# Two token blocks through w_in by Strassen's scheme, seven products instead of eight, with twelve weight slots

## The chip, the cores and the metric

One core of a Trainium2 chip runs the kernel. The metric is the device time of one execution in microseconds (us); the median of several runs is given. TensorE (PE in the rows) multiplies matrices into PSUM, which has eight banks of 128 x 512 fp32 values; VectorE (DVE), ScalarE (ACT) and GpSimd (POOL) do the rest, and SyncE (SP) issues the DMAs.

## The reference

Attention over four batches of eight heads, with 32 global tokens that see everything and 512 local ones that see a window of 32 and the global ones, gives 2176 tokens of 512 features. These go through two layers of the same form, in fp32:

```python
x = np.ascontiguousarray(attn_out.transpose(0, 2, 1, 3)).reshape(B * S, H * D)   # 2176 x 512
...
h = x @ w_in                 # 512 x 2048
r = np.maximum(h, 0.0)
g = r * r
return (g @ w_out).astype(np.float32)    # 2048 x 512
```

## The kernel before

Every operation is first entered in a plan (`add`: engine, estimated cost, priority, what it reads and writes). `order` then plays the plan through with its estimates, each engine taking the ready operation of the lowest priority number, and the operations are issued in the order that comes out. So each engine has one fixed order. Dependences follow the order in which operations were added: who writes a buffer waits for all who read it before.

Products are made precise by splitting: a value is stored as a high part (`xh`, `gh`, `whi`) in a rounded fp32 type (F32R) and the rest (`xl`, `gl`, `wlo`), and each product takes three matmuls: high by high, high weight by low value, low weight by high value (lines 509 to 511 and 534 to 536).

The tokens stand in five blocks of 256, 512, 512, 512 and 384 columns, numbered 0 to 4. A layer is cut into four waves of 512 hidden features; there are eight waves in all (`lw`), numbered 0 to 7, and a wave takes every block through `moe`. For each of four groups f of 128 hidden features, four groups k of 128 input features are accumulated in a bank (h or S, four of these); then `r` = relu on ScalarE, its square to `gh` on ScalarE, the same to `gf` on VectorE (line 523) and `gl` = `gf` - `gh` on VectorE (`minus`, line 218). Then w_out: four groups d of output features by four f, accumulated in four banks (Y, PT, PT, O), and added to `y` by VectorE (line 547; in a layer's first wave ScalarE copies instead). The last wave of the first layer splits y into the next layer's `xh` and `xl`, the last wave of the second stores y.

Weights come as 64-bit patterns in chunks of 512 KB, eight in a wave (four of w_in, four of w_out). `weight` loads one into `wraw` (there is one such buffer) and turns it into fp32 in `wt` by four VectorE operations and an absolute value that VectorE or ScalarE makes (lines 466 to 478); ScalarE writes the high part into a slot (line 484), and VectorE or GpSimd the low part (`minus`, 'wl'). There are 16 slots, two waves' worth; eight of them take the room of attention's buffers once attention is done (`arena`).

Attention (`pair`, 32 of them, and `glob`, 8) fills x block by block, and wave 0 of the first layer runs in between. From wave 1 on, banks and slots of attention are free for the rest. In the waves 1 to 6 the blocks run in the order 1, 2, 4, 0, 3, in the last in the order 1, 2, 3, 4, 0. Two activations can be under way (`r`, `gf`: two buffers each). The settings are in `CFG`: letters say which engine takes an operation (A ScalarE, D VectorE, P GpSimd), in turn.

Of the kernel before, what the change touches and what calls it, by code (L numbers as in the profile page):

```python
# [10 lines left out]
F32 = mybir.dt.float32  # L11
# [20 lines left out]
NSLOT = 16  # L32
CFG = {'EARLY': 8,
 'ck': 'PPP',
 'cq': 'P',
 'lo': 'D',
 'nm': 'AD',
 'ev': 'A',
 'yc': 'AA',
 'wl': 'DDPP',  # L40
 'gl': 'D',
 'xh': 'AADA',
 'glob': [5, 5, 13, 17, 19, 27, 31, 37],
 'w0': -1.361,
 'w1': 684422.049,
 'moe': [341.089, 23.225, 54.691, -112.195, -211.616],
 'step': [0.2638, 0.5671, 0.1425, 0.013, 0.2305],
 'NK': 3,
 'NQ': 3,
 'wa': 'DAA',  # L50
 'lid': -317.614,
 'lmk': -11.49,
 'gbuf': '01',
 'lead': 14.017,
 'NM': 2,
 'NS': 3,
 'NPT': 5,
 'NV': 2,
 'NR': 2,
 'NG': 2,  # L60
 'NWR': 1,
 'NWT': 2,
# [17 lines left out]
class Op:  # L80
    __slots__ = ("eng", "cost", "fn", "prio", "seq", "deps", "users", "left", "ready", "start", "end", "tail", "lock")


class Plan:
# [8 lines left out]
    def add(self, eng, cost, prio, fn, reads=(), writes=(), tail=0.0, lock=False):  # L93
        op = Op()
        op.eng, op.cost, op.prio, op.fn, op.tail, op.lock = eng, cost, prio, fn, tail, lock
        op.seq = len(self.ops)
# [23 lines left out]
    def order(self):  # L120
# [7 lines left out]
        done, dma, dmas, cols, port = [], 0.55, [], {}, {}  # L128
        while len(done) < len(self.ops):
# [14 lines left out]
            if e == "PE":  # L144
                n = int(t / TICK)
                if cols.get(n - 1, 0.0) < 3060:
                    op.end += op.cost * 0.95
# [23 lines left out]
        return done  # L171

# [14 lines left out]
def kernel(ctx: ExitStack, tc: tile.TileContext, kl, ql, vl, gk, gv, win, wout, msk, idn, out):  # L187
# [27 lines left out]
    def minus(key, prio, out_, a, b, n, reads, writes):  # L215
        get = lambda v: v() if callable(v) else v
        if pick(key) == "D":
            add("DVE", dve(n), prio, lambda: nc.vector.tensor_tensor(  # L218
                out=get(out_), in0=a, in1=get(b), op=ALU.subtract), reads, writes, lock=True)
        else:  # L220
            add("Pool", 0.25 + 0.0021 * n, prio, lambda: nc.gpsimd.tensor_tensor(  # L221
                out=get(out_), in0=a, in1=get(b), op=ALU.subtract), reads, writes)
# [14 lines left out]
    NR, NG, NWR, NWT = (CFG[k] for k in ("NR", "NG", "NWR", "NWT"))  # L237
    rt = tiles(big, "r", NR, [128, 512])
    gft = tiles(big, "gf", NG, [128, 512])
# [22 lines left out]
    late_opened = []  # L262

    def open_late():
        if not late_opened:
# [3 lines left out]
            for j in range(NSLOT - EARLY):  # L269
                whi.append(lp.tile([128, 512], F32R, name=f"whi{EARLY + j}"))  # L270
                wlo.append(lp.tile([128, 512], F32R, name=f"wlo{EARLY + j}"))

    bank = {k: ps.tile([128, 512], F32, name=k) for x in ("h", "Y", "S", "PT", "O") for k in CFG[x]}
    cnt = {"S": 0, "PT": 0, "g": 0, "h": 0, "Y": 0, "r": 0, "gf": 0}
# [10 lines left out]
    def pair(j, prio):  # L285
# [31 lines left out]
        add("PE", 0.86, P(), scores, A + (M, ML, HQ, LQ), tuple(sk))  # L317
        pbs = []
        ok = CFG["O"][j % len(CFG["O"])]
        for e in range(2):  # L320
# [31 lines left out]
            add("PE", 0.468, P(), trans, A + (("s", sb, 0), ("s", sb, 1), "ident"), (tk,))  # L352
# [13 lines left out]
        add("PE", 1.03, P(), pv, A + (("pt", pbs[0]), ("pt", pbs[1]), ("v", vb)), (ok,))  # L366
        b, c0 = UNIT_POS[u]
        split_out(b, [h2], xh[b][:, h2, c0:c0 + 256], xl[b][:, h2, c0:c0 + 256], ok, bank[ok][:, 0:256], 256, P)
# [8 lines left out]
    def glob(n, prio):  # L377
# [16 lines left out]
        for e in range(2):  # L394
# [7 lines left out]
            add("PE", 0.96, P(), scores, A + (GK,), (sk,))  # L402
# [20 lines left out]
        def trans():  # L423
# [3 lines left out]
        add("PE", 0.49, P(), trans, A + (GP, "ident"), (t1,))  # L427
        copy("ev", P(), kt[:, 0:512], bank[t1], 512, A + (t1,), (GK,), psum=True)
        add("PE", 0.15, P(), lambda: nc.tensor.transpose(bank[t2][0:32, 0:128], p[:, 512:544], ident),
            A + (GP, "ident"), (t2,))  # L430
# [12 lines left out]
        add("PE", 1.645, P(), pv, A + (GK, GV), (ok,))  # L443
# [7 lines left out]
    def weight(c, prio):  # L451
        w, r = divmod(c, 8)
        src = (win if r < 4 else wout)[4 * w + r % 4]
        slot, rb, tb = c % (NSLOT), c % NWR, c % NWT
        late = slot >= EARLY
        R, T = ("wraw", rb), ("wt", tb)
        q = [prio]

        def P():
            q[0] += 1e-3  # L460
            return q[0]

        low, high, t = wraw[rb][:, :, 0], wraw[rb][:, :, 1], wtmp[tb]
        tf = t.bitcast(F32)
        load(prio, wraw[rb].rearrange("p c t -> p (c t)"), src.bitcast(U32), 524288, (), (R,))
# [14 lines left out]

        def hi():
            if late:
                open_late()
            nc.scalar.activation(out=whi[slot], in_=tf, func=AF.Copy)  # L484

        W = (("w", slot),) + ((("arena",) if c < NSLOT else ()) if late else ())
# [198 lines left out]
```

## Time and profile before

| | |
|---|---|
| median of 3 runs | 904.36 us (904.07 to 904.84) |
| the profiled execution | 904.31 us, its span 902.5 us |
| TensorE busy | 888.0 us (98%) |
| VectorE, ScalarE, GpSimd busy | 577.3, 405.2, 80.7 us |
| read from HBM, written | 62.54 MB, 4.46 MB |

The span goes from the first instruction to the last; the 1.81 us between it and the execution's time lie around it. Busy times count how long an engine had an instruction under way. Matmuls overlap, so their lengths are longer than the distance from one to the next, and the distance is what counts. The same holds for VectorE's operations.

### The profile page before, as it was taken

The page shows a single profiled execution, that of the slowest core. Times are in us where ns is not written, and L with a number is a line of the kernel's source. Part 1 is how long each engine was busy: PE and PEld are TensorE (multiplying, and loading weights), DVE is VectorE, ACT ScalarE, POOL GpSimd, SP SyncE. Part 2 cuts the span into 40 slices and gives each one's busy share as a digit, 9 for nine tenths or more (in the row PEclk, how much of TensorE's full clock was granted, in tenths as well). Part 3 has the DMA queues.
Part 4 walks back from the last instruction along what each step waited for, and adds up shares of the span by engine and source line. Part 5 has one row for each costly group of instructions (what it writes and reads, how often), then busy time and mean ns, then how long its engine had stood idle before and what let it go on. Part 6 is the DMA issues. An engine that isn't in the chain of part 4 may idle for free.

```text
span 902.5 us, 14362 instructions
## 1 busy us (share of the span) xinstructions
PE 888.0 (98%) x5416; PEld 765.8 (85%) x5416; DVE 577.3 (64%) x1396; ACT 405.2 (45%) x933; POOL 80.7 (9%) x108
## 2 busy tenths in 40 slices
PE   6999999999999999999999999999999999999998
PEld 4878777778888988898889888998899889988888
DVE  6999989655567777765776675356645763333343
ACT  5989788755433333333344444454313332222221
POOL 2322221100110011001000001000100110000000
PEclk9999999999999999999999999999999999999999
DMA  9768634210222222221110012002200210001111
GB/s 313 249 196 251 193 106 134 81 32 1 70 71 64 59 89 71 70 70 47 52 66 24 24 60 80 25 24 71 69 25 2 70 47 1 1 1 48 47 47 59
DMA packets 28069, 67.92 MB, mean 75 GB/s; under 512 B 3168, under 2 KB 12512, under 8 KB 28000
## 3 DMA queue, kind: packets, MB, share of 16 engines
q1 hardware_dynamic: 28000, 67.01, 23.6%
q8 instruction: 42, 0.69, 0.3%
q14 instruction: 27, 0.22, 0.1%
HBM read 62.54 MB, written 4.46 MB: 74 GB/s over the span
## 4 chain that ended last, share of the span: by engine, by line
PE 92%; DVE 4%; ACT 2%; DMA 2%; issue 0%; SPq 0%; ACTq 0%
PE h L509 8%; PE h L510 7%; PE h L511 7%; PE S L510 6%; PE S L509 6%; PE S L511 6%; PE PT L534 6%; PE PT L536 6%; PE PT L535 6%; PE Y L534 5%; PE Y L536 4%; PE Y L535 4%; PE O L534 3%; PE O L535 3%; PE O L536 3%; PE O L362 3%
## 5 line engine op out<-in xcount | busy, mean ns | idle before, releaser
L519 ACT ACTIVATE r<-h 128x512 f32<-128x512 f32 (+2 forms) x88 | 46.8, 533 | 220.1 <-PE h L511 219.9
L509 PE MATMUL h<-xh,whi 128*128 128x512 f32 (+2 forms) x352 | 130.2, 370 | 0.7 <-DVE gf L523 0.7
L510 PE MATMUL h<-xl,whi 128*128 128x512 f32 (+2 forms) x352 | 126.4, 359 | 0.0
L511 PE MATMUL h<-xh,wlo 128*128 128x512 f32 (+2 forms) x352 | 126.1, 358 | 0.0
L218 DVE TENSOR_TENSOR gl<-gf,gh 128x512 fp32r<-128x512 f32 (+2 forms) x160 | 99.5, 623 | 21.5 <-ACT gh L521 10.4
L534 PE MATMUL PT<-gh,whi 128*128 128x512 f32 (+2 forms) x288 | 102.6, 356 | 0.0
L511 PE MATMUL S<-xh,wlo 128*128 128x512 f32 (+2 forms) x288 | 102.6, 356 | 0.0
L536 PE MATMUL PT<-gh,wlo 128*128 128x512 f32 (+2 forms) x288 | 102.6, 356 | 0.0
L510 PE MATMUL S<-xl,whi 128*128 128x512 f32 (+2 forms) x288 | 102.6, 356 | 0.0
L509 PE MATMUL S<-xh,whi 128*128 128x512 f32 (+2 forms) x288 | 102.6, 356 | 0.0
L535 PE MATMUL PT<-gl,whi 128*128 128x512 f32 (+2 forms) x288 | 102.6, 356 | 0.0
L523 DVE SCALAR_TENSOR_TENSOR gf<-h,r 128x512 f32<-128x512 f32 (+2 forms) x88 | 53.5, 609 | 73.5 <-ACT r L519 73.2
L521 ACT ACTIVATE gh<-r 128x512 fp32r<-128x512 f32 (+2 forms) x160 | 90.4, 567 | 6.4 <-PE Y L536 2.4
L221 POOL TENSOR_TENSOR wlo<-wt,whi 128x512 fp32r<-128x512 f32 x32 | 43.6, 1364 | 521.5 <-ACT whi L484 521.5
L534 PE MATMUL Y<-gh,whi 128*128 128x512 f32 (+2 forms) x208 | 76.6, 368 | 0.0
L509 PEld LDWEIGHTS h<-xh,whi 128*128 128x128 f32 x352 | 66.4, 189 | 11.1 <-DVE gf L523 0.9
L536 PE MATMUL Y<-gh,wlo 128*128 128x512 f32 (+2 forms) x208 | 74.6, 359 | 0.0
L535 PE MATMUL Y<-gl,whi 128*128 128x512 f32 (+2 forms) x208 | 74.6, 359 | 0.0
L511 PEld LDWEIGHTS h<-xh,wlo 128*128 128x128 f32 x352 | 66.5, 189 | 8.6
L510 PEld LDWEIGHTS h<-xl,whi 128*128 128x128 f32 x352 | 66.5, 189 | 7.8 <-DVE xl L373 0.2
L547 DVE TENSOR_TENSOR y<-y,Y 128x512 f32<-128x512 f32 (+2 forms) x30 | 18.2, 606 | 84.3 <-PE Y L536 84.2
L519 ACT ACTIVATE r<-S 128x512 f32<-128x512 f32 (+2 forms) x72 | 38.4, 533 | 67.8 <-PE S L511 65.2
(79 smaller groups left out, 1758.9 us busy)
## 6 DMA issues: line engine op xcount, KB each, us to landing
wraw<-win SPq DMA_DIRECT2D x32, 512.0 KB, 3.5
wraw<-wout SPq DMA_DIRECT2D x32, 512.0 KB, 3.5
v<-vl SPq DMA_DIRECT2D x32, 224.0 KB, 2.9
rk<-kl SPq DMA_DIRECT2D x32, 192.0 KB, 3.8
y<-gk SPq DMA_DIRECT2D x8, 672.0 KB, 6.1
y<-gv SPq DMA_DIRECT2D x8, 640.0 KB, 8.2
rq<-ql SPq DMA_DIRECT2D x32, 128.0 KB, 3.1
out<-y SPq DMA_DIRECT2D x12, 256.0 KB, 2.1
```

Source lines behind the costliest of these rows:

```text
L218: add("DVE", dve(n), prio, lambda: nc.vector.tensor_tensor(out=get(out_), in0=a, in1=get(b), op=ALU.subtract), reads, writes, lock=True)
L221: add("Pool", 0.25 + 0.0021 * n, prio, lambda: nc.gpsimd.tensor_tensor(out=get(out_), in0=a, in1=get(b), op=ALU.subtract), reads, writes)
L362: nc.tensor.matmul(out=bank[ok][64 * e:64 * e + 64, 128 * t:128 * t + 128], lhsT=vt[vb][:, 128 * k + 64 * e:128 * k + 64 * e + 64], rhs=pt ...
L509: nc.tensor.matmul(out=hp, lhsT=hi, rhs=xh[b][:, k, :], start=k == 0, stop=False)
L510: nc.tensor.matmul(out=hp, lhsT=hi, rhs=xl[b][:, k, :], start=False, stop=False)
L511: nc.tensor.matmul(out=hp, lhsT=lo, rhs=xh[b][:, k, :], start=False, stop=k == KD - 1)
L519: add("Activation", act(nb), P(), lambda r=r, hp=hp: nc.scalar.activation(out=r, in_=hp, func=AF.Relu), (hk,), (("r", ri),))
L521: add("Activation", act(nb) + 0.04, P(), lambda r=r, a=a: nc.scalar.activation(out=a, in_=r, func=AF.Square), (("r", ri),), (("gh", f),))
L523: add("DVE", dve(nb), P(), lambda r=r, hp=hp, gf=gf: nc.vector.scalar_tensor_tensor(out=gf, in0=hp, scalar=0.0, in1=r, op0=ALU.max, op1=AL ...
L534: nc.tensor.matmul(out=o, lhsT=hi, rhs=gh[f][:, 0:nb], start=f == 0, stop=False)
L535: nc.tensor.matmul(out=o, lhsT=hi, rhs=gl[f][:, 0:nb], start=False, stop=False)
L536: nc.tensor.matmul(out=o, lhsT=lo, rhs=gh[f][:, 0:nb], start=False, stop=f == 3)
```

## The change

In waves 1 to 7 blocks 1 and 2 no longer go through `moe` each for itself but together through `wino`, W in the orders. The two blocks, two halves of the input features (k 0, 1 and k 2, 3) and a pair of f make a 2 x 2 by 2 x 2 product of blocks; `products` computes it by seven products of six matmuls each, in Winograd's form of Strassen's scheme. For that

- four sums of the two blocks' x are made (`tsums`): T1 takes the place of block 2's first half, T2 to T4 have tiles of their own. It runs once before wave 1, from `xh` + `xl`, and once before the second layer, from y;
- each pair of w_in chunks gets four half sums (`sums`), which fill two more slots, split as the chunks are. A wave holds 4 + 4 + 4 = 12 slots, and there are 12;
- a bank B accumulates product after product, and is copied out in between (`keep`, ScalarE); two other banks take the products that are added to those copies (`plus`, VectorE). Three of the four results of a pair are thus in `r` buffers, of which there are now three, and go through `activate` with `staged` (VectorE squares in place, ScalarE copies to `gh`); `gf` is gone;
- w_out of blocks 1 and 2 is accumulated for two f at a time (`second`) and added to y twice in a wave.

The slots are given out from a list of free ones, in the order in which they are released. The orders of blocks are 340W, 3W04, W403, 4W30, W043, 0W43 and 3W40 for the waves 1 to 7. The planner now counts a cost for a change between kinds of matmul (`switch`), and many settings of attention are others: which engine casts, normalises and converts, how many buffers there are, and in which order wave 0, the loads and the `glob`s come. `visit` and `after` only rearrange code. Unchanged lines and most of the first part are left out:

```diff
-NSLOT = 16
+NSLOT = 12
+PB = (1, 2)
...
+ 'tl': 'D',
+ 'tp': [495.69, 306.05],
+ 'order': ['340W', '3W04', 'W403', '4W30', 'W043', '0W43', '3W40'],
...
- 'nm': 'AD',
+ 'nm': 'APA',
...
- 'wl': 'DDPP',
+ 'wl': 'DDDD',
...
- 'xh': 'AADA',
- 'glob': [5, 5, 13, 17, 19, 27, 31, 37],
...
+ 'xh': 'AAA',
+ 'glob': [6, 7, 13, 15, 19, 26, 27, 29],
...
- 'NQ': 3,
- 'wa': 'DAA',
...
+ 'NQ': 2,
+ 'wa': 'ADDA',
...
- 'NPT': 5,
+ 'NPT': 2,
...
- 'NR': 2,
- 'NG': 2,
+ 'lag': 6,
+ 'NR': 3,
...
- 'NWT': 2,
+ 'NWT': 3,
...
+    def sums(f0, f1, slots, P, arenas):
+
+        (t0, T0), (t1, T1) = f0, f1
+        half = lambda t, i: t[:, 256 * i:256 * i + 256]
+        for out_, a, b, op, rd, wr in (
+                (half(t0, 0), half(t0, 0), half(t1, 0), ALU.subtract, (T1,), T0),
+                (half(t1, 0), half(t1, 0), half(t1, 1), ALU.add, (), T1),
+                (half(t1, 1), half(t1, 1), half(t0, 0), ALU.subtract, (T0,), T1),
+                (half(t0, 1), half(t0, 1), half(t1, 1), ALU.subtract, (T1,), T0)):
+            add("DVE", dve(256), P(), lambda out_=out_, a=a, b=b, op=op: nc.vector.tensor_tensor(
+                out=out_, in0=a, in1=b, op=op), rd, (wr,), lock=True)
+        for s, (t, T) in zip(slots, ((t1, T1), (t0, T0))):
+            split(s, t, T, P, arenas[s])
...
+        for p in range(2):
+            t = [chunk("in", 2 * p + i) for i in range(2)]
+            ss = [slot() for _ in range(2)]
+            sums(t[0], t[1], [s for s, _ in ss], P, dict(ss))
+            res["sum"].append([s for s, _ in ss])
+            for i in range(2):
+                chunk("out", 2 * p + i)
...
+        if staged:
+            r, R = src, S
+            add("DVE", dve(nb), P(), lambda: nc.vector.scalar_tensor_tensor(
+                out=r, in0=r, scalar=0.0, in1=r, op0=ALU.max, op1=ALU.mult), (), (R,), lock=True)
+            add("Activation", act(nb) + 0.04, P(), lambda: nc.scalar.activation(out=a, in_=r, func=AF.Copy),
+                (R,), (("gh", f),))
...
+        def keep(i):
+            copy("sg", P(), s[i], B, nb, (kb,), (G[i],), psum=True)
+
+        def plus(i, hk, hp):
+            add("DVE", dve(nb), P(), lambda: nc.vector.tensor_tensor(out=s[i], in0=s[i], in1=hp, op=ALU.add), (hk,), (G[i],))
+
+        product(kb, B, f0, 0, x(b0, 0), True)
+        keep(0)
+        product(ka, A, f0, 2, x(b0, 2), True)
+        plus(0, ka, A)
+        activate(P, 0, nb, s[0], G[0], True)
+        product(kb, B, sa, 2 - 2, t(2), False, False) if False else product(kb, B, sa, 2, t(2), False)
+        keep(1)
+        product(kc, C, sa, 0, t(1), True)
+        product(kb, B, sb, 0, t(3), False)
+        keep(2)
+        plus(2, kc, C)
+        product(kb, B, f1, 2, t(4), False)
+        activate(P, 1, nb, B, kb, False)
+        product(kc, C, sb, 2, x(b1, 2), False)
+        plus(1, kc, C)
+        rest = lambda: (activate(P, 3, nb, s[2], G[2], True), activate(P, 2, nb, s[1], G[1], True))
...
+        r0 = products(W, 0, P)
+        r0()
+        release(*W["sum"][0])
+        st_ = lambda p: (layer, wave == 0 and p == 0, wave == WAVES - 1 and p == 1)
+        second(P, PB[0], (0, 1), o[0:2], True, True, st_(0))
+        r1 = products(W, 1, P)
+        release(*W["sum"][1])
+        second(P, PB[1], (2, 3), o[0:2], True, True, st_(0))
+        r1()
+        second(P, PB[0], (0, 1), o[2:4], True, True, st_(1))
+        second(P, PB[1], (2, 3), o[2:4], True, True, st_(1))
+        if free:
+            release(*W["in"], *W["out"])
...
+                whole(s0, S0, b1, 2 + i)
+                whole(s1, S1, b1, i)
+                tt(s0, s0, s1, ALU.subtract, (S1,), S0)
+                split_t(3, i, s0, S0)
+                whole(s2, S2, b0, i)
+                tt(s1, s1, s2, ALU.subtract, (S2,), S1)
+                split_t(1, i, s1, S1)
+                tt(s0, s0, s2, ALU.add, (S2,), S0)
+                split_t(2, i, s0, S0)
+                whole(s1, S1, b0, 2 + i)
+                tt(s1, s1, s0, ALU.subtract, (S0,), S1)
+                split_t(4, i, s1, S1)
```

## Rows read from the trace of the kernel before

**Rows 1.** The page: busy time of each engine; engines of the last chain
```profile
PE 888.0 (98%) x5416; PEld 765.8 (85%) x5416; DVE 577.3 (64%) x1396; ACT 405.2 (45%) x933; POOL 80.7 (9%) x108
...
PE 92%; DVE 4%; ACT 2%; DMA 2%; issue 0%; SPq 0%; ACTq 0%
```

**Rows 2.** Windows of stage one: stretch, length, then busy us of each engine
```profile
0.00:27.50 27.50, 18.85 (x127) 14.94 (x127) 19.70 (x78) 15.43 (x43) 6.22 (x15) 1.00 0.83 280
27.50:100.00 72.50, 71.69 (x821) 58.06 (x819) 69.14 (x295) 65.10 (x206) 18.68 (x33) 1.00 0.73 225
100.00:220.00 120.00, 118.43 (x988) 94.89 (x987) 85.73 (x333) 88.37 (x257) 17.82 (x32) 1.00 0.31 92
220.00:244.50 24.50, 24.50 (x121) 21.70 (x120) 15.87 (x30) 11.99 (x23) 2.58 (x2) 1.00 0.16 45
```

**Rows 3.** Windows, columns as in the group before: waves 1, 4 and 7
```profile
244.50:338.00 93.50, 93.50 (x488) 82.91 (x487) 66.68 (x116) 34.27 (x62) 8.03 (x6) 1.00 0.24 73
...
525.00:618.00 93.00, 93.00 (x480) 81.83 (x479) 50.38 (x87) 40.08 (x75) 5.76 (x4) 1.00 0.15 46
...
805.00:898.70 93.70, 93.70 (x482) 82.40 (x481) 36.79 (x61) 22.05 (x40) 0.00 (x0) 1.00 0.12 43
```

**Rows 4.** Timeline of TensorE, wave 1: start us, length us, line, output<-inputs
```profile
253.34 0.39 PE L509 MATMUL S<-xh,whi 128*128 128x512 f32 x1
...
254.70 0.39 PE L509 MATMUL S<-xh,whi 128*128 128x512 f32 x1
```

**Rows 5.** Waits of TensorE, line <- releaser: us in total, times, longest us
```profile
PE S L314 <- POOL hq L211: 4.8, 1, 4.8
PE S L314 <- DVE mn L326: 3.0, 1, 3.0
PE h L509 <- DVE gf L523: 0.7, 1, 0.7
```

**Rows 6.** Timeline, the end: the last matmul
```profile
898.71 0.28 PE L536 MATMUL O<-gh,wlo 128*128 128x256 f32 x1
```

**Rows 7.** Timeline of VectorE: operations of 512 columns, and one of 256
```profile
473.36 0.68 DVE L547 TENSOR_TENSOR y<-y,Y 128x512 f32<-128x512 f32 x1
...
476.96 0.68 DVE L547 TENSOR_TENSOR y<-y,O 128x512 f32<-128x512 f32 x1
...
494.22 0.43 DVE L218 TENSOR_TENSOR gl<-gf,gh 128x256 fp32r<-128x256 f32 x1
```

**Rows 8.** Timeline of VectorE, weight conversions in wave 1: L466 begins, L478 ends
```profile
247.13 0.43 DVE L466 TENSOR_SCALAR wt<-wraw 128x512 uint32<-128x512 uint32 x1 [2.12 <-DMA wraw<-wout]
...
319.81 0.69 DVE L478 SCALAR_TENSOR_TENSOR wt<-wraw,wt 128x512 f32<-128x512 f32 x1
324.13 0.43 DVE L466 TENSOR_SCALAR wt<-wraw 128x512 uint32<-128x512 uint32 x1 [0.15 <-DMA wraw<-wout]
...
338.11 0.42 DVE L466 TENSOR_SCALAR wt<-wraw 128x512 uint32<-128x512 uint32 x1
```

**Rows 9.** Lines by shape, 220 to 902 us: count, busy us, mean ns
```profile
L203 ACT ACTIVATE y<-PT 128x512 f32<-128x512 f32 x6 | 3.6, 598 | 0.5
```

**Rows 10.** Lines by shape, 0 to 220 us, columns as before
```profile
L203 ACT ACTIVATE s<-s,sm 128x224 f32<-128x224 f32 x64 | 30.1, 476 | 4.4 <-DVE sm L337 3.2 <-DVE lq L302 0.4 <-DVE gmx L408 0.4
L208 DVE TENSOR_SCALAR s<-s,sm 128x224 f32<-128x224 f32 x64 | 22.4, 351 | 0.4
L203 ACT ACTIVATE xh<-O 128x256 fp32r<-128x256 f32 x24 | 9.1, 377 | 10.3 <-PE O L362 8.9 <-DVE gmx L408 1.4
```

**Rows 11.** Timeline: TensorE behind a ScalarE copy, ScalarE behind a matmul
```profile
14.62 0.57 ACT L203 ACTIVATE pt<-PT 112x512 f32<-112x512 f32 x1
15.25 0.91 PE L362 MATMUL O<-pt,v 112*64 112x128 f32 x6 [0.62 <-ACT pt L203]
...
343.19 0.39 PE L511 MATMUL h<-xh,wlo 128*128 128x512 f32 x1
343.62 0.60 ACT L519 ACTIVATE r<-h 128x512 f32<-128x512 f32 x1 [0.93 <-PE h L511]
```

More of the change, by code (lines that the diff above doesn't have):

```diff
@@ L80 @@
 class Op:
-    __slots__ = ("eng", "cost", "fn", "prio", "seq", "deps", "users", "left", "ready", "start", "end", "tail", "lock")
+    __slots__ = ("eng", "cost", "fn", "prio", "seq", "deps", "users", "left", "ready", "start", "end", "tail", "lock", "mode")
 class Plan:
@@ L481, in hi, with split @@
+    def split(slot, tf, T, P, arena):
         def hi():
[L482 removed]
+            if slot >= EARLY:
                 open_late()
             nc.scalar.activation(out=whi[slot], in_=tf, func=AF.Copy)
[L486 to L487 removed]
+        add("Activation", act(512) + 0.04, P(), hi, (T,), (("w", slot),) + arena)
         minus("wl", P(), lambda: wlo[slot], tf, lambda: whi[slot].bitcast(F32), 512, (T,), (("w", slot),))
[L491 removed]
+    fresh = list(range(NSLOT))
@@ L492, in moe @@
+    def moe(W, layer, wave, b, prio, late, step=1e-3, free=False):
         nb = NB[b]
@@ new lines, in moe, with products, product @@
+            activate(P, f, nb, hp, hk, False)
+        second(P, b, range(4), W["out"], late, not late, (layer, wave == 0, wave == WAVES - 1))
+        if free:
+            release(*W["in"], *W["out"])
+    tkey = lambda n, i: ("x", PB[1], i) if n == 1 else ("T", n, i)
+    th = lambda n, i: xh[PB[1]][:, i, :] if n == 1 else tt_[n - 2][0][:, i, :]
+    tl = lambda n, i: xl[PB[1]][:, i, :] if n == 1 else tt_[n - 2][1][:, i, :]
+    def products(W, p, P):
+        b0, b1 = PB
+        nb = NB[b0]
+        c3 = 3 * pe_r(nb)
+        f0, f1 = W["in"][2 * p:2 * p + 2]
+        sa, sb = W["sum"][p]
+        kb, ka, kc = (take("h", CFG["h"] + CFG["S"]) for _ in range(3))
+        B, A, C = (bank[k][:, 0:nb] for k in (kb, ka, kc))
+        def product(hk, hp, slot, k0, X, start):
+            for i in range(2):
+                xhi, xlo, key = X(i)
+                add("PE", c3, P(), lambda i=i, xhi=xhi, xlo=xlo: three(
+                    hp, wv(whi, slot)[:, k0 + i, :], wv(wlo, slot)[:, k0 + i, :], xhi(), xlo(), start and i == 0, i == 1, not start),
+                    (("w", slot), key), (hk,))
+        x = lambda b, k0: (lambda i: (lambda: xh[b][:, k0 + i, :], lambda: xl[b][:, k0 + i, :], ("x", b, k0 + i)))
+        t = lambda n: (lambda i: (lambda: th(n, i), lambda: tl(n, i), tkey(n, i)))
+        s, G = zip(*[(t[:, 0:nb], g) for t, g in (staging() for _ in range(3))])
+        def keep(i):
[18 more added lines that the diff above has]
+        rest = lambda: (activate(P, 3, nb, s[2], G[2], True), activate(P, 2, nb, s[1], G[1], True))
+        return rest
@@ new lines, in wino, with P @@
+    def wino(W, layer, wave, prio, step=1e-3, free=False):
+        q = [prio]
+        def P():
+            q[0] += step
+            return q[0]
+        o = W["out"]
+        r0 = products(W, 0, P)
[9 more added lines that the diff above has]
+        second(P, PB[1], (2, 3), o[2:4], True, True, st_(1))
+        if free:
+            release(*W["in"], *W["out"])
@@ L576 @@
     GPOS = CFG["glob"]
-    for c in range(8):
-        weight(c, CFG["w0"] + CFG["w1"] * c)
+    W = weights(0, CFG["w0"], CFG["w1"])
     for j in range(NI // 2):
```

300 lines of the change are left out of this document (190 added, 110 removed).

## The prediction

> **What bounds the kernel now.** I read the shares of the page first. TensorE is busy for 888.0 of 902.5 us, VectorE (DVE) for 64%, ScalarE (ACT) for 45%, and the chain that ended last lies on TensorE for 92% of its length [rows 1]. A share is an average, so next I cut the span into stretches. Two stages show. Up to 244.5 us attention runs mixed with wave 0 of the first layer; VectorE is at 95% and ScalarE at 90% between 27.5 and 100 us, and TensorE still has 71.69 of 72.50 us [rows 2]. From 244.5 to 898.7 us run waves 1 to 7, about 93.5 us each, and there TensorE's busy time equals the stretch in each of the seven (the first, fourth and last stand), while VectorE falls from 66.68 us to 36.79 us, the last wave having no weights left to convert [rows 3]. A busy TensorE could still be a slow one, so I looked at single matmuls: from 253.34 to 254.70 us lie six 512-column matmuls, 0.2267 us each [rows 4]. A wave is 96 matmuls for each of five blocks, and three of the blocks have 512 columns, so 288 x 0.2267 = 65.3 us of a wave are such matmuls, run without a gap. The waits of TensorE confirm it: the longest are 4.8 and 3.0 us in attention, the only one on a w_in product is 0.7 us [rows 5]. So from 244.5 us on the kernel is as long as its matmuls, and only fewer matmuls, or a TensorE that has to wait, change it. The last matmul starts at 898.71 us; the 3.8 us behind it are the last add and the stores [rows 6].
>
> **What goes away.** For two blocks of 512 tokens the old w_in step has 2 blocks x 4 f x 4 k x 3 = 96 matmuls. In the new one `products` runs once for each pair of f, with seven products of 2 x 3 matmuls: 2 x 42 = 84. That is 12 fewer in a wave, 84 in the seven waves with a W. At 0.2267 us [rows 4] this is 84 x 0.2267 = 19.04 us, all on the path. The w_out matmuls are as many as before (16 passes of 3 for a block, split in two halves), of the same shape. The Trainium skill, "TensorE: Matmul & The Clock Gate", section "Back-to-back issue gap", gives 512/2.4 + 2.5 = 216 ns for such a matmul; by that the gain would be an estimated 18.1 us. The trace's spacing is 5% longer, and the sum goes by the trace.
>
> **What VectorE gets.** A 512-column operation takes 0.60 us from start to start: six of them start between 473.36 and 476.96 us, where the seventh starts [rows 7]. The durations of single rows, 0.68, overlap. For each W wave come: three adds of a product to a kept sum (`plus`) in each pair, 6 x 0.60 = 3.6 us; eight more adds into y, since w_out of blocks 1 and 2 now ends twice, 8 x 0.60 = 4.8; the low halves of four more chunks of weights that GpSimd (POOL) did, 4 x 0.60 = 2.4; eight 256-column sums of weights, at most 8 x 0.43 = 3.4 [rows 7]; and the low halves of four summed slots, 2.4. Together 16.6 us. What was there is 36.8 us without weights, and 66.68 - 36.79 = 29.9 us for the twelve conversions that begin in wave 1, so 2.5 us each [rows 3, 8]: 36.8 + 8 x 2.5 + 16.6 = 73.4 us in a wave of (898.7 - 244.5)/7 - 12 x 0.2267 = 93.46 - 2.72 = 90.7, or 81%. Wave 1 of the old kernel had 71% with no idle TensorE. So VectorE stays under the bound and this is costed at nothing; the cover is 17 us of VectorE's idle time in a wave. Once, before wave 1, `tsums` adds 8 + 8 + 8 operations, 14.4 us; its slots for T rotate with the activations (three r buffers), so block 3 of wave 1 can't be activated before it is done. It falls around 220 to 255 us, where VectorE is idle for 8.6 us of 24.5 [rows 2] and block 3's 48 w_in matmuls (10.9 us) can run ahead of their activations over four PSUM banks. If that cover failed, up to 14.4 - 8.6 = 5.8 us would be on the path. The second `tsums` (16 operations, 9.6 us) has three whole blocks behind it.
>
> **What ScalarE, GpSimd and SyncE get.** ScalarE keeps three products in a pair and does three Relus fewer, which cancels; the four summed slots cost 4 x 0.60 = 2.4 us [rows 9] in waves where it has at most 40 of 93 us [rows 3]: nothing. GpSimd loses the low halves and gets a third of the normalisations. SyncE issues the same 64 weight loads, no more.
>
> **The attention stage** has other settings. 64 normalisations of 351 ns leave VectorE (22.4 us); about 85 instead of 64 lie on ScalarE at 476 ns, +10.0 us, and about 10 casts of x at 377 ns, +3.8 us [rows 10]. Buffers shrink (pt 5 to 2, rq 3 to 2). On the gain side the bound is TensorE's idle time behind its first matmul: 27.5 - 18.85 - 4.84 = 3.8 us, then 0.81 and 1.57, in all 6.2 us [rows 2, 5]. On the loss side it is ScalarE's 13.8 us for the part of the stage in which it is near full, 100 of 220 us: 6.3 us. I take -1 us, nearer to the 2.4 us of idle time after 27.5 us than to either end: VectorE, the fuller engine, is relieved by more than ScalarE takes.
>
> **New waits.** Product B goes through one bank four times in a pair and is read in between (`keep`). Behind the first two reads six matmuls into another bank follow, 1.36 us. Behind the third, the next product into B follows at once, and C waits for its own `plus`, which needs that copy. The turn costs: ScalarE starts 0.20 us behind the end of the last matmul (343.19 + 0.23 to 343.62), copies in 0.60, and a matmul started 0.06 us behind a copy's end (14.62 + 0.57 to 15.25): 0.86 us [rows 9, 11]. TensorE has other work for it, the first product of the next pair in the fourth bank or w_out of the block before; uncovered it is 14 x 0.86 = 12.0 us. The 12 slots are the other new wait. A W wave fills all of them, so weights of the next wave wait for this wave's readers; the old kernel, with 16, converted twelve chunks in wave 1 alone [rows 3, 8]. I take 2 us for all this, one turn at the start of each of the first two W waves, where the conversions are latest; the bounds are 0 and 12.0.
>
> **Sum.** Profiled time 904.31 us (span 902.5 plus 1.81 around it; the median of the runs is 904.36, the same). 904.31 - 19.04 - 1 + 2 = 886.3 us.
>
> **Rivals.**
> 1. *The bank turns are not covered.* Against it: three streams (pair, next pair, block before) lie ready, and in the old waves none of the ScalarE turns shows on TensorE [rows 3, 5]. For it: banks h and S are four, and a pair holds three of them. It gives 904.31 - 19.04 - 1 + 12.0 = 896.3. The Trainium skill, "Perfetto Trace Analysis", section "Optimizing Tensor Performance", speaks for this rival: independent matmul groups should rotate through PSUM banks, so that reading out one overlaps the next. The trace agrees with it, as the old groups rotate over four banks and no such wait shows [rows 5]; the new scheme returns to one bank. Chance 0.10.
> 2. *The weights come late, and it is slower.* Place: the boundaries into waves 1 and 2, the first with `tsums` in VectorE's way, the second because wave 1 ends with W, whose pairs hold the slots to the end. Price: with one raw buffer twelve conversions follow one another from 247.13 to 338.11 us, 7.58 us each, of which 3.6 us pass between the end of the last read and the next load's first use (320.5 to 324.13) [rows 8]. If the last four chunks are converted behind the boundary, the fourth is there after 30.3 us; block 3 needs it after its 48 w_in matmuls and 36 of w_out, 84 x 0.2267 = 19.0 us. That is 11.3 us a boundary, covered by the 42 matmuls (9.5 us) of the W behind it if these run first. It decides if both boundaries stay uncovered: 904.31 - 19.04 - 1 + 22.6 = 906.9. Against it: half of a wave's chunks have free slots before its boundary. Chance 0.11, with cases between it and rival 1.
> 3. *The attention stage grows* by its bound, with the small buffers: 904.31 - 19.04 + 6.3 + 2 = 893.6. Chance 0.08.
> 4. *The scheme saves no matmuls* (sums recomputed, or products split): then the matmul count would not fall by 84 and the time stays near 904. By the count of the code, 0.02.
>
> **How the numbers follow.** The forecast has 0.69; its range is 904.31 - 19.04 - 6.2 = 879.1 to about 892. The range of 8 in 10 reaches to rivals 1 and 3 and stops short of rival 2: 879 to 899. A difference of 0.2% (1.8 us) is about what can be told from no change. Faster: 0.69 + 0.10 + 0.08 less 0.03 for mixtures of rivals = 0.84. Same: 0.05 (rival 4 and a mild rival 2). Slower: 0.11.
>
> **What would show it.** Right: 84 matmuls of 512 columns fewer; each wave about 90.7 us; TensorE's waits in the waves under a few us; VectorE about 73 us in a wave. Rival 1: TensorE waiting for ScalarE copies, some fourteen times 0.9 us. Rival 2: gaps of several us ahead of w_in or w_out matmuls in wave 1 or 2, released by the whi or wlo writes. Rival 3: attention ending later, and wave 1 beginning later than 244.5 us. Wrong altogether: if wave 1 begins on time and waves still take 93 us with no gaps.

## Result, and the profile after

The changed kernel takes 895.14 us (median; 893.89 to 896.30) where the kernel before took 904.22 beside it: a ratio of 0.9899, 95% interval 0.9882 to 0.9916. It is 9.1 us faster. The forecast was 886.3, a gain of 18. The sign held, and so did the range of 8 in 10 (879 to 899); the time lies 3 us above the forecast's own range (879.1 to about 892), and the gain came out at half.

The page of the changed kernel, against [rows 1]: 84 matmuls fewer, as the prediction had counted, and VectorE up from 577 to 686 us.

```profile
PE 871.2 (98%) x5332; PEld 752.9 (84%) x5332; DVE 685.5 (77%) x1584; ACT 428.9 (48%) x996; POOL 64.6 (7%) x119
...
PE 92%; DVE 3%; DMA 2%; ACT 2%; issue 1%; SPq 0%; POOL 0%; POOLq 0%; DVEq 0%; ACTq 0%
```

Windows of the changed kernel over waves 1, 3 and 7 (stretch, length, busy us of PE, PEld, DVE, ACT, POOL, then granted clock, DMA share, GB/s), against [rows 3]:

```profile
251.30:342.00 90.70, 89.68 (x464) 78.79 (x463) 74.19 (x132) 34.00 (x62) 0.00 (x0) 1.00 0.11 34
...
432.80:523.50 90.70, 90.70 (x471) 80.12 (x470) 83.92 (x155) 41.80 (x77) 0.00 (x0) 1.00 0.14 43
...
795.70:888.30 92.60, 92.60 (x478) 81.47 (x476) 49.85 (x83) 23.06 (x43) 0.00 (x0) 1.00 0.13 49
```

The waves now have about 90.7 us, as forecast, and in the windows of all seven TensorE is idle only in the first, for 1.02 us. So the gain of the waves is there, and the missing time lies ahead of them, in stage one (attention and wave 0). Two marks part the kernel: the first matmul of wave 1 that follows the last one of wave 0, and the last matmul of all. The timeline of TensorE in the changed kernel:

```profile
242.95 0.39 PE L575 MATMUL h<-xh,whi 128*128 128x512 f32 x1
...
251.97 0.39 PE L575 MATMUL h<-xh,whi 128*128 128x512 f32 x1
...
888.21 0.28 PE L577 MATMUL O<-gh,wlo 128*128 128x256 f32 x1
```

and the first of the marks in the kernel before (the second is [rows 6]):

```profile
248.54 0.39 PE L509 MATMUL h<-xh,whi 128*128 128x512 f32 x1
```

In the kernel before, 18 matmuls of wave 1 had run ahead of that mark, here only the three from 242.95 us. With these early matmuls counted to wave 1, at 0.2267 us each, wave 1 begins at 248.54 - 4.08 = 244.46 us before and at 251.97 - 0.68 = 251.29 after: **stage one grew by 6.83 us**. From there to the last matmul it is 654.25 us before and 636.92 after: **the waves shrank by 17.33 us**, which is 19.04 less 1.7. Together that is -10.5 us, by one profile of each. The medians differ by 9.1: the profiled run of the changed kernel is the fastest of its four, so in the median run stage one grew by an estimated 8.2.

Where stage one lost it: the windows over 27.5 to 100 us of the changed kernel,

```profile
27.50:60.00 32.50, 29.78 (x311) 24.52 (x310) 24.55 (x107) 26.09 (x84) 9.96 (x18) 0.95 0.64 198
60.00:100.00 40.00, 39.74 (x440) 32.07 (x438) 35.99 (x146) 36.44 (x109) 13.85 (x24) 1.00 0.70 231
```

and the first stretch in the kernel before:

```profile
27.50:60.00 32.50, 31.82 (x386) 26.66 (x384) 31.11 (x135) 30.27 (x97) 8.77 (x15) 1.00 0.77 239
```

Between 27.5 and 60 us TensorE, VectorE and ScalarE all do less than before (ScalarE 26.09 against 30.27 us), and the granted clock is 0.95. So something else holds them. The waits of TensorE in the changed kernel (us in total, times, longest), against [rows 5]:

```profile
PE S L330 <- DVE mn L342: 6.3, 3, 5.3
PE S L330 <- POOL hq L226: 4.2, 1, 4.2
PE O L378 <- DMA v<-vl: 2.7, 1, 2.7
PE Y L575 <- ACT y L218: 2.5, 4, 0.7
PE S L575 <- DVE r L599: 1.0, 1, 1.0
```

The first is the landing of the masks at the start (3.0 us before), the third a v load that lands late. Of the fourth, three waits of 0.69 us are turns through the one bank Y0 in w_out of block 3, wave 0, at 232.69, 236.40 and 240.10 us; one of 0.47 us, at 112.95 us, is on the block of 256 columns. (Block 3 has four groups of 12 matmuls in that bank, so three turns; the expectations below count four.) The last line is the activation of block 3 in wave 1, behind the T sums. No line names the `keep` copies. The third sits in a queue of transfers. The timeline of SyncE's issues there (changed kernel):

```profile
41.45 0.33 SPq L298 DMA_DIRECT2D y<-gk  x1
41.83 0.42 SPq L298 DMA_DIRECT2D y<-gv  x1
...
44.18 0.33 SPq L298 DMA_DIRECT2D wraw<-win  x1
44.60 0.80 SPq L298 DMA_DIRECT2D v<-vl  x1
```

The timeline of VectorE, at the first reader of the weights:

```profile
53.41 0.43 DVE L488 TENSOR_SCALAR wt<-wraw 128x512 uint32<-128x512 uint32 x1 [3.12 <-DMA wraw<-win]
```

The timeline of TensorE, at the reader of v:

```profile
54.11 1.98 PE L378 MATMUL O<-pt,v 112*64 112x128 f32 x16 [2.72 <-DMA v<-vl]
```

The weights issued at 44.18 us are usable at 53.41, the v issued at 44.60 at 54.11. VectorE stands 3.12 us at a weight conversion with attention's operations queued behind it. The kernel before had such a queue too: two global pairs were issued ahead of this weight load, which took 7.5 us to land (at 49.03 by the trace), against 9.2 here. But there VectorE came to these weights only at 57.12 us, and waited for nothing:

```profile
41.57 0.39 SPq L282 DMA_DIRECT2D wraw<-win  x1
...
57.12 0.41 DVE L466 TENSOR_SCALAR wt<-wraw 128x512 uint32<-128x512 uint32 x1
```

In the changed kernel VectorE was ready for them at 50.29 us (53.41 - 3.12). So the load lands 4.4 us later, and its reader comes 6.8 us sooner; it is the two together that make the wait.

And the 2.72 us of TensorE are not all; windows of the changed kernel, columns as above:

```profile
54.00:56.00 2.00, 1.89 (x16) 1.60 (x16) 1.97 (x11) 0.88 (x3) 0.70 (x1) 0.50 0.08 32
56.00:57.00 1.00, 1.00 (x6) 0.99 (x5) 0.51 (x4) 0.88 (x4) 0.02 (x1) 0.50 0.00 0
57.00:58.00 1.00, 1.00 (x5) 0.73 (x4) 0.54 (x3) 1.00 (x5) 0.26 (x1) 0.81 0.89 223
```

Behind the wait the granted clock is 0.50, which is 1.2 GHz, for a little over 3 us. At half speed that is an estimated 1.6 us more. By this, 4.3 of the 6.8 us lie in this one place.

The turns at 232 to 240 us are a second place. Each takes 0.85 us from matmul to matmul beyond the usual spacing (239.02 to 240.10 us, less 0.23). In the kernel before, six of the 18 early matmuls stand between each two of the four groups, and no wait shows there. With three early matmuls instead of 18, the three turns lie open: an estimated 2.6 us.

### The profile page after: what moved, and what is told of

It is laid out like the page before. It is cut to its first block, busy times and chain, and to the rows that moved or that the text cites. A ratio compares the mean times of both kernels' runs of the same rounds, so it can differ in the third digit from the quotient of the medians.

```text
span 892.0 us, 14332 instructions
## 1 busy us (share of the span) xinstructions
PE 871.2 (98%) x5332; PEld 752.9 (84%) x5332; DVE 685.5 (77%) x1584; ACT 428.9 (48%) x996; POOL 64.6 (7%) x119
## 4 chain that ended last, share of the span: by engine, by line
PE 92%; DVE 3%; DMA 2%; ACT 2%; issue 1%; SPq 0%; POOL 0%; POOLq 0%; DVEq 0%; ACTq 0%
PE h L575 7%; PE h L576 7%; PE h L577 7%; PE PT L575 6%; PE PT L577 6%; PE PT L576 6%; PE S L575 6%; PE S L577 6%; PE S L576 6%; PE Y L575 5%; PE Y L577 4%; PE Y L576 4%; PE O L378 4%; PE O L575 3%; PE O L577 3%; PE O L576 3%
## 5 line engine op out<-in xcount | busy, mean ns | idle before, releaser
L575 PE MATMUL h<-xh,whi 128*128 128x512 f32 (+2 forms) x298 | 108.2, 363 | 0.0
L576 PE MATMUL h<-xl,whi 128*128 128x512 f32 (+2 forms) x298 | 105.3, 353 | 0.0
L233 DVE TENSOR_TENSOR gl<-r,gh 128x512 fp32r<-128x512 f32 (+2 forms) x160 | 96.8, 608 | 9.9 <-ACT gh L591 7.9
L524 ACT ACTIVATE whi<-wt 128x512 fp32r<-128x512 f32 x92 | 57.3, 627 | 60.9 <-DVE wt L500 38.9
L233 DVE TENSOR_TENSOR wlo<-wt,whi 128x512 fp32r<-128x512 f32 x92 | 62.8, 686 | 26.1 <-ACT whi L524 25.9
L575 PE MATMUL S<-xh,whi 128*128 128x512 f32 (+2 forms) x230 | 80.2, 349 | 1.0 <-DVE r L599 1.0
L577 PE MATMUL S<-xh,wlo 128*128 128x512 f32 (+2 forms) x230 | 80.1, 348 | 0.0
L576 PE MATMUL S<-xl,whi 128*128 128x512 f32 (+2 forms) x230 | 80.1, 348 | 0.0
L596 ACT ACTIVATE r<-h 128x512 f32<-128x512 f32 (+2 forms) x67 | 34.3, 512 | 73.4 <-PE h L577 73.0
L597 ACT ACTIVATE gh<-r 128x512 fp32r<-128x512 f32 (+2 forms) x118 | 63.9, 542 | 10.4 <-PE O L577 6.6
L347 ACT ACTIVATE s<-s,mn 128x224 f32<-128x224 f32 x128 | 60.3, 474 | 17.0 <-DVE mn L342 16.1
```

Source lines behind the costliest of these rows:

```text
L233: add("DVE", dve(n), prio, lambda: nc.vector.tensor_tensor(out=get(out_), in0=get(a), in1=get(b), op=ALU.subtract), reads, writes, lock=True)
L347: add("Activation", 0.48, P(), lambda t=t, sb=sb: nc.scalar.activation(out=st[sb][:, t, :], in_=st[sb][:, t, :], func=AF.Exp, bias=mn[sb][ ...
L575: nc.tensor.matmul(out=out_, lhsT=hi, rhs=xhi, start=start, stop=False, skip_group_check=again)
L576: nc.tensor.matmul(out=out_, lhsT=hi, rhs=xlo, start=False, stop=False, skip_group_check=again)
L577: nc.tensor.matmul(out=out_, lhsT=lo, rhs=xhi, start=False, stop=stop, skip_group_check=again)
L596: add("Activation", act(nb), P(), lambda: nc.scalar.activation(out=r, in_=src, func=AF.Relu), (S,), (R,))
```

## The experiments

"Mark" is the first of the two marks above, "waves" the time from it to the last matmul, both of the one profiled run. The changed kernel has 251.97 and 636.24.

| run | median us | ratio to before, 95% | mark | waves |
|---|---|---|---|---|
| changed kernel | 895.14 | 0.9882 to 0.9916 | 251.97 | 636.24 |
| e1 masks first | 892.49 | 0.9845 to 0.9886 | 251.60 | 636.47 |
| e2 third v buffer | 893.67 | 0.985 to 0.9897 | 251.50 | 636.26 |
| e3 four banks | 894.84 | 0.9833 to 0.9915 | 252.69 | 636.48 |
| e4 all three | 892.65 | 0.9838 to 0.9891 | 253.38 | 636.48 |
| e5 globals behind weights | 889.59 | 0.9819 to 0.9852 | 247.38 | 636.37 |
| e6 two globals cut | 888.90 | 0.9815 to 0.9845 | 246.70 | 636.48 |
| e7 Strassen undone | 911.28 | 1.0061 to 1.0091 | 250.30 | 653.67 |
| e8 20 low parts doubled | 934.40 | 1.0313 to 1.0344 | 249.59 | 677.09 |
| e9 globals and masks | 889.45 | 0.9822 to 0.9851 | 246.23 | 636.23 |
| e10 old settings | 896.59 | 0.9904 to 0.9934 | 249.03 | 643.17 |
| e11 low parts of W doubled | 910.98 | 1.006 to 1.009 | 253.01 | 652.59 |
| e12 the others doubled | 914.78 | 1.0103 to 1.0144 | 248.77 | 657.13 |

All but e7 and e10 keep the changed kernel's order of instructions on every engine, but for the operation named, so the same matmul can be compared from run to run; e7 and e10 were planned anew. The edits are shown abridged.

**One wait at a time.** The first four took TensorE's visible waits of stage one away singly, then together.

```
e1:  place("masks", ahead of ("v", 0))                # SyncE's third load
e2:  vt = tiles(ap_, "v", 3, [112, 512]); ("v", 6) ahead of ("gk", 3)
e3:  yr = ["Y0", "PT0", "PT1", "O0"] if b == 3 and not late else yk
e4:  e1 + e2 + e3
```

> The changed kernel with every engine's order as planned, but the load of the masks issued third instead of eighth on SyncE. In the changed kernel the first score reduction waits for the masks until 10.75 us (9.12 us in the kernel before), and TensorE's second scores start at 11.61 instead of 9.98 us. Theory (the attention stage grew in three places: the late masks, a late load of v at 51 to 54 us, four turns of one bank at 232 to 241 us): the reduction starts 3 to 4 us earlier, at about 7 us, and all behind it comes 1.6 to 4 us earlier; time 891 to 893.5. Rival (the start is bound by the casts and exponentials behind the masks): second scores move, wave 1 doesn't; time within 0.5 us of the changed kernel's 895.1.

Measured 892.49 us. The median is 2.7 us lower and within the theory's range, though the runs of the two kernels overlap (891.12 to 894.81, 893.89 to 896.30). In the profiled run the mark moved by 0.4 us alone: in the first 27.5 us TensorE gained 1.3 us of work (18.42 against 17.09), and between 60 and 100 us it did 0.6 us less. Nor is the gain at the start surely the edit's. TensorE's second scores start at 10.20 us here, and in e12, where the masks' load is left in its place, they start sooner still:

```profile
10.04 1.08 PE L331 MATMUL S<-hk,hq 64*128 64x224 f32 x2 [3.83 <-DVE mn L343]
```

So e1 does not show what the masks' place is worth.

> The changed kernel with a third buffer for v, and the seventh load of v issued ahead of the fourth pair's load of global keys instead of behind it; all else in the planned order. In the changed kernel that load needs 9.4 us to land, TensorE idles 2.7 us for it and then has a stretch of matmuls at twice their spacing. Theory: the idle time and the slow stretch go, 3 to 4.5 us; time 890.5 to 892.5. Rival (the transfer only moves and delays the global keys instead): the gap shows up at the scores of the global tokens, time within 1 us of 895.1.

Measured 893.67, between the two forecasts. The 2.7 us for v are gone, and in their place stands this wait of TensorE:

```profile
PE S L427 <- DVE mn L343: 1.7, 1, 1.7
```

These are scores behind an attention reduction on VectorE, and VectorE is where it was, at the weight conversion (52.79 us, after 2.27 us of waiting). The clock stays at 1.00 this time, and at 60 us the run is 2.0 us ahead of the changed kernel, matmul for matmul. At 75 us it is 0.2 ahead. In between, the same thing happens once more: the next weight load is issued at 62.05 us, behind the next global pair (60.19 and 60.56 us), and VectorE waits for it:

```profile
69.93 0.43 DVE L489 TENSOR_SCALAR wt<-wraw 128x512 uint32<-128x512 uint32 x1 [2.20 <-DMA wraw<-wout]
```

In the changed kernel this wait is 0.47 us, in e1 1.50. This second queue is what takes back most of what e1 and e2 had won before it.

> The changed kernel with w_out of block 3 in wave 0 written to the four banks Y0, PT0, PT1, O0 in turn instead of four times to Y0; planned order. In the changed kernel TensorE waits there for ScalarE's copy of y, 0.85 us each time between 232 and 241 us. Theory A (these turns are a cost of their own): 2.5 to 3.5 us go; time 891.6 to 892.6. Theory B (VectorE's chain, the twenty-four tsums operations at 245 to 262 us, sets when wave 1 can go on): the gaps go, and the wait of TensorE for VectorE's activation at 262 us grows by as much, time 894 to 895.5.

Measured 894.84, as theory B had it, but not by its mechanism. The turns are gone, and from 231 to 242 us this run gains 2.9 us on the changed kernel. Then 1.7 us are lost at the first matmul of wave 1, for whose wait the profile names no releaser:

```profile
243.42 0.47 PE L576 MATMUL h<-xh,whi 128*128 128x512 f32 x1 [1.28 <-issue]
```

VectorE ends an activation of block 4, behind a weight conversion, at 243.32 us, so that is likely the cause. Only 0.3 us more are lost behind the T sums, and 1.0 us stays. It does not show in the mark, because this profiled run had come to the place 2.0 us later than the changed kernel, by waits that the edit does not touch. A turn cost what the forecast had priced it at, 0.85 against 0.86 us, but taking the three away kept only a third of their time.

> The three edits together: masks early, third v buffer, four banks. If the attention stage's three places are what the forecast missed (it had wave 1 start 1 us earlier, it started 6.8 us later), the sum is 7 to 10 us: time 885 to 888, and wave 1 starts at about 243 us as in the kernel before. If VectorE's chain before wave 1 takes the place of the bank turns, 888 to 890.

Measured 892.65, 4.7 us above the end of the first range and 2.7 above that of the second. Waits of TensorE in this run:

```profile
PE S L331 <- POOL hk L226: 4.2, 1, 4.2
...
PE S L427 <- DVE mn L343: 2.7, 1, 2.7
```

Two windows of it, behind the last of these waits:

```profile
56.00:58.00 2.00, 2.00 (x8) 1.48 (x8) 1.38 (x7) 1.48 (x7) 0.45 (x1) 0.50 0.20 63
58.00:60.00 2.00, 2.00 (x7) 1.54 (x5) 0.53 (x3) 1.11 (x3) 0.45 (x1) 0.50 0.30 92
```

The masks' wait has become one on the first keys, whose load they now precede, and the wait at 54 us is there again by way of VectorE, with the half clock behind it. The theory that three separate waits make up the loss fell; the four banks gained 0.9 us here again. What the four runs have in common is the late weight load, for which VectorE waits 2.62, 2.27, 3.21 and 3.29 us, so the next two took that.

**The transfers between 37 and 53 us.**

```
e5:  place(("gk", 3), ahead of ("rq", 10)); place(("gv", 3), ahead of ("rq", 10))
e6:  c2, c3 = (1088, 128) if n in (2, 3) else (0, 1280)
     load(k[:, c2:1344], gk[n][:, c2:1344]); load(v[:, 0:c3], gv[n][:, 0:c3])
```

> In the changed kernel the loads of global pair 3 (gk and gv, 1.34 MB) are issued at 41.45 and 41.83 us, ahead of the weight load of 44.18 us, which lands only at about 53.4; VectorE, whose order is fixed, stands 3.12 us for it, with the attention operations queued behind. Here these two loads are issued behind the weight load and the seventh v load, nothing else is moved. Theory A (DMA backlog and a fixed order make the loss at 50 to 60 us): the weight load and v land some 4 us sooner, VectorE's 3.1 us wait and TensorE's 2.7 us wait at 54 us go, and wave 1 begins 3 to 4 us earlier: 891 to 892 us. Theory B (another limit of the attention stage stands right behind): the wait goes, but the time stays within 1 us of the changed kernel's 895.1.

Measured 889.59 us, 5.6 lower by the medians and 4.6 by the marks, for moving two loads past four others; that is 1.4 us below the range of theory A. The timeline of VectorE in this run, at the first reader of the weights:

```profile
49.74 0.42 DVE L489 TENSOR_SCALAR wt<-wraw 128x512 uint32<-128x512 uint32 x1
```

Windows of it:

```profile
27.50:60.00 32.50, 32.37 (x376) 26.88 (x378) 27.94 (x122) 28.78 (x90) 12.33 (x21) 1.00 0.70 211
...
54.00:56.00 2.00, 2.00 (x25) 1.68 (x23) 1.77 (x9) 1.54 (x5) 0.53 (x2) 1.00 0.64 158
```

Its two marks, in the timeline of TensorE:

```profile
247.38 0.39 PE L576 MATMUL h<-xh,whi 128*128 128x512 f32 x1
...
883.75 0.28 PE L578 MATMUL O<-gh,wlo 128*128 128x256 f32 x1
```

The conversion starts 3.7 us sooner with no wait, TensorE is busy for 32.37 of the 32.5 us, and the clock stays at 1.00. Matmul for matmul, the run is 0.5 us ahead of the changed kernel at 49 us, before the move can tell, 4.8 at 58 us and 4.6 at the mark, 190 us later. So the move is worth 4.1 us by the profiles and 5.6 by the medians.

> Left out: of global pairs 2 and 3 only the query columns of gk and a tenth of gv are loaded, so these pairs work on stale keys and values; every instruction stays. This takes 2.3 MB out of the transfers between 37 and 53 us. Theory A (backlog): the weight load issued at 44.2 us lands in under 6 us instead of 9.2, VectorE does not wait, and the loss of TensorE between 50 and 60 us falls from 4.8 us to about 1; wave 1 begins 3 to 5 us earlier: 890 to 892 us. Theory B (the stage is set by VectorE and ScalarE at 90% and more): the loss comes back before 120 us and the time stays within 1 us of 895.1.

Measured 888.90: without 2.3 MB of these transfers it is only 0.7 us less than with the two loads moved, and in the profiles these 0.7 us are there in the first 12 us already, before any of the loads in question. So the move took nearly all that the backlog cost. Theory A holds in both runs, with times 1.1 to 1.4 us below its ranges.

**The scheme without the rest.**

```
e7:  order = CFG["order"][lw - 1].replace("W", "12")   # no sums, no tsums
```

> The attention stage, its settings and the 12 slots stay as changed; blocks 1 and 2 go through w_in one after the other with eight products again, and the sums of weights and of activations fall away. Theory A (the scheme gives its full 84 matmuls, 19.0 us, and costs the waves some 1.7 us): 895.1 + 19.0 - 1.7 = about 912.5 us, range 911 to 914; slower than before, by the attention stage's 6.8 us and what is left. Rival (the scheme gives much less than its matmuls, the new settings cost little): 900 to 906 us.

Measured 911.28, as theory A had it. Its marks:

```profile
250.30 0.39 PE L572 MATMUL h<-xh,whi 128*128 128x512 f32 x1
...
903.97 0.28 PE L574 MATMUL O<-gh,wlo 128*128 128x256 f32 x1
```

The waves have 653.67 us, 17.4 more than with the scheme, and the same as in the kernel before (248.54 less the 15 more early matmuls, 3.40 us, to 898.71 is 653.57). So 12 slots and the new settings cost the waves nothing, and the whole is slower than before by 6.8 us by the medians, all of it in stage one. (By the marks stage one has grown by 5.2 us here; the profiled run is the fastest of four, 1.7 us under the median.) The scheme itself is not needed for the loss.

**VectorE's reserve.**

```
e8:   gl written twice, all 20 of a wave, from wave 1 on
e11:  only the 8 of the W step
e12:  only the 12 of the other three blocks
```

> From wave 1 on each low part of an activation (gl, 20 in a wave, 12.0 us of VectorE's time) is written twice with the same values; nothing else is moved. Theory A (VectorE lies beside TensorE up to its whole idle time of some 7 to 24 us in a wave): waves 1, 2, 4, 5, 6 and 7 stay within 1 us of 90.7; wave 3, with the second set of T sums at 83.9 us, comes to some 94 to 96 us and grows by 3 to 5 us; 898 to 901 us in all. Rival (inside a W step VectorE is already the limit or the turns through it are on the path): each of the seven waves grows by 3 us or more, the time is 916 us or more.

Measured 934.40: theory A fell, and the time lies in the rival's range. Three windows of this run, 100 us each:

```profile
350.00:450.00 100.00, 95.69 (x477) 80.58 (x477) 91.75 (x168) 33.76 (x61) 0.00 (x0) 1.00 0.17 53
450.00:550.00 100.00, 94.33 (x472) 80.79 (x471) 94.31 (x171) 41.33 (x77) 0.00 (x0) 0.98 0.12 37
550.00:650.00 100.00, 94.95 (x462) 79.82 (x461) 80.27 (x145) 42.79 (x81) 0.00 (x0) 0.98 0.16 48
```

TensorE is now idle for 4 to 6 us in each, in the third too, where VectorE has 20 us to spare.

> All 20 low parts of a wave written twice added 12.0 us to VectorE's work and made a wave 5.8 us longer. Here only the 8 low parts of the W step are written twice (5.4 us a wave). Theory A (what counts is VectorE's total in a wave: it can't use its last 10 per cent of idle time): at 80 of 90.7 us on the mean most of it is hidden, the waves grow by 4 to 12 us in all, 898 to 907 us. Rival (the turns of the W step through VectorE are on the path): most of the 40 us come back with these eight alone, 920 us or more.

> The counterpart: only the 12 low parts of the three blocks outside the W step are written twice (6.6 us a wave). Theory A (VectorE's total in a wave): as with the W step's own, 898 to 908 us. Rival (the turns of the W step are on the path, the other blocks have slack): the time stays within 3 us of the changed kernel, 893 to 898 us.

Measured 910.98 and 914.78; both prices are above what theory A had, and neither rival came. Over half of TensorE's waits in the waves of e11 are one line:

```profile
PE Y L577 <- DVE gl L233: 5.5, 9, 1.3
```

By the marks the waves grew by 16.4 and 20.9 us, and by 40.9 with both. At 0.60 us an operation, e11 added 8 x 0.60 x 7 = 33.6 us to VectorE, and e12 made it busy for 42 us more in the waves, so about half of what is added is paid, wherever in the wave it stands. (In e8 two stretches of the waves and in e12 one, of a little over 3 us each, ran at half clock behind such waits, an estimated 1.6 us apiece.) A full VectorE does not explain that, as the third window shows; the turns through it do: the second of a pass's three matmuls in w_out waits for a `gl` that stands behind other work in a fixed order. The order was not planned again for the added work; a new plan might pay less, which no run here shows.

**Old settings with the new scheme.**

```
e10:  attention's engine choices, buffer counts, places of the global pairs and
      due times of the kernel before; waves, sums and 12 slots of the changed one
```

> The Strassen waves with 12 slots as changed, but attention with the settings of the kernel before (its choice of engines, its buffer counts, its places of the global pairs, its order). Theory A (the scheme is worth 17.4 us in the waves and the 6.8 us lost in attention come from the new settings alone): 904.5 - 17.4 = 887 us, range 886 to 889. Rival (the new settings are what gets the T sums and the weights of wave 1 ready in time, with 12 slots): a gap of 4 to 7 us ahead of block 3's or the W step's matmuls in wave 1 takes the place of the loss, 891 to 895 us.

Measured 896.59: the rival in kind, 1.6 us above its range. The timeline of TensorE in wave 1 of this run:

```profile
259.14 0.79 PE L574 MATMUL S<-xh,whi 128*128 128x512 f32 x1 [5.14 <-ACT whi L523]
```

The timeline of ScalarE, at what it waited for:

```profile
258.46 0.63 ACT L523 ACTIVATE whi<-wt 128x512 fp32r<-128x512 f32 x1 [0.58 <-DVE wt L499]
```

A window behind the wait:

```profile
259.00:261.00 2.00, 1.86 (x4) 1.13 (x5) 1.34 (x4) 1.34 (x4) 0.00 (x0) 0.50 0.68 219
```

The weights for the third f of w_in are late by 5.14 us, because their conversion shares VectorE with the T sums, and the half clock follows again. The new settings are therefore not a plain loss: they bring wave 1 its weights in time. The mark is 2.9 us earlier than in the changed kernel, and not 6.8: with attention's old settings stage one is still 3.9 us longer than in the kernel before. Part of that is the open turns: here too only three matmuls of wave 1 run early, and TensorE waits 0.86 and 0.69 us at two turns, at 233.46 and 237.17 us. In e7 it is three early matmuls and three turns of 0.69 us. What these runs share with the changed kernel is the 12 slots and block 3 ahead in wave 1; which of these takes the early matmuls away was not tested, and the rest stays unexplained.

**The two best moves together.**

```
e9:  e5 + e1
```

> The move of global pair 3's loads behind the weight load (889.6 us alone) and the masks' load as the third one on SyncE (892.5 us alone) together, nothing else moved. Theory A (the two losses lie in different places, the masks' at 9 to 12 us and the backlog at 37 to 58 us, and are paid one after the other): the first mask reduction comes some 1.6 us sooner and all of it stays, 887.5 to 888.5 us. Theory B (what is won at the start is waited away before 100 us, as when the masks were moved alone in the profiled run): 889 to 890 us.

Measured 889.45 against 889.59 us: theory B by the medians. In the profiled run, the fastest of the four, the mark is 1.2 us earlier than in e5, so a small gain is not ruled out. e5, the smaller edit, is 1.6% faster than the kernel before and 0.6% faster than the changed one.

## Why the forecast came out at half

- **84 matmuls, 19.04 us: right.** The count fell by 84, a wave has 90.7 us, and undoing the scheme alone gave 17.4 us back. By the 216 ns that the Trainium skill ("TensorE: Matmul & The Clock Gate", "Back-to-back issue gap") gives for a matmul by itself, the saving would be an estimated 18.1. The spacing in [rows 4] was the better base: 17.4 and the stop in wave 1 (next point) make 18.7.
- **New waits, +2 us: right in size by luck, wrong in place.** It was 1.6 to 1.7 us. The forecast took it for bank turns at the start of the first two W waves. Instead TensorE stops once, at 262 us, for block 3's activation behind the first T sums: 1.0 us idle, 1.3 us with the slower start behind it. The working had named this place with a bound of 5.8 us and put it at nothing. The remaining 0.4 us is spread thinly and not located.
- **Bank turns (rival 1): covered in the waves, open ahead of them.** No wait on a `keep` copy shows. The rule of the Trainium skill, "Perfetto Trace Analysis" ("Optimizing Tensor Performance"), to rotate independent groups through banks, bore out in part at another spot: with three turns on Y0 given other banks, e3 won 2.9 us and kept 1.0. The prediction did not ask what covered these turns in the kernel before, which is the 18 early matmuls.
- **VectorE, 73.4 us in a wave: right.** Waves 1, 2, 4, 5 and 6 have 74.19, 78.67, 66.74, 74.70 and 71.98, mean 73.3; wave 3 with the second T sums 83.92. "Costed at nothing" was right too. The reason was not: 17 us of idle time are no cover of 17 us. e11 paid for about half of 4.8 us a wave.
- **Attention, -1 us: wrong; it was +6.8.** This is the term that failed. It was bounded by engines' busy time, ScalarE's 13.8 us at the worst. The loss end of 6.3 us came near the truth by luck: a fuller ScalarE did not occur, as between 27.5 and 60 us it does less than before, and in e5 TensorE is busy for 32.37 of these 32.5 us with the same settings. The step that was missing is the one for SyncE and its readers: the prediction counted the weight loads ("the same 64 weight loads, no more") and did not ask when the largest loads of the kernel, 1.34 MB for a global pair, would be issued under the new places and fewer buffers, which weight load stands behind them, and when VectorE's fixed order would come to that load. The loads of two pairs, issued between 31.9 and 36.9 us before, are now issued between 37.1 and 41.8; the weight load behind them moved from 41.57 to 44.18 us, and its reader came at 50.29 instead of 57.12. e5 shows that cause and its price, 4.1 to 5.6 us.
- **Rival 3** (893.6 us) was the nearest in time and place, with a chance of 0.08, but it laid the growth to ScalarE's bound and the small buffers. **Rival 2** (weights late at the first boundary) did not come in the changed kernel; e10 shows it at the first boundary, 5.14 us, under the old settings. **Rival 4** is out by the count.
- **Open:** with e5, wave 1 begins at 246.70 us (early matmuls counted), still 2.2 us later than before. The three open turns, an estimated 2.6 us, are of that size, but e5 with four banks was not run, and by e3 only 1.0 us of them would stay. What the masks' place is worth is not shown.

## What to carry to other kernels

When a change comes with new settings, follow the largest transfers first: when each is issued, which small load is queued behind it, and when that load's reader comes. Here moving two loads was worth 5.6 us, beside the 17.3 us that the scheme won. An engine's idle time need not be a reserve where its order is fixed: price added work at something between nothing and its full length, and test it by doubling an operation. And before taking one wait away, ask what is late next: e2 removed the wait that the profile named, and the next load in the queue took most of the time back.

## What was not expected of the hardware

- Short waits were followed by the half clock. After 2.72 us without a matmul in the changed kernel, and after 5.14 us in e10, TensorE was granted 0.50 for 3 us and more; in e8 and e12 the same came after single waits of 2.16 us in the waves. In e2, after 1.67 us, the clock stayed at 1.00. The first wait thus cost about 1.6 times what its line said, by the estimate above; against e5, matmul for matmul, the half clock cost the changed kernel 1.5 us.
- The same instructions in stage one had their mark between 248.77 and 253.01 us in four profiled runs (the changed kernel, e8, e11, e12), while the waves of one kernel repeat to 0.3 us. With the backlog taken out (e5, e6, e9) the marks lie at 246.23 to 247.38, and e5's times within 888.74 to 889.99 us. How much a full queue of transfers costs differs from run to run. e11 and e12 have the same instructions up to there and are 0.2 us apart at 49 us, but 4.2 at 61 us, as these windows of e11 and then of e12 show:

```profile
52.00:59.00 7.00, 6.27 (x30) 5.21 (x31) 4.74 (x21) 3.68 (x13) 1.31 (x3) 0.51 0.21 61
...
52.00:59.00 7.00, 7.00 (x87) 5.94 (x85) 6.40 (x28) 6.49 (x20) 2.46 (x4) 1.00 0.31 87
```
